# Fused attention and ResMLP: globals of the first two batches by indirect DMA, odd V chunks of batch 0 by VectorE, four score buffers, gated loads and a new order table

## The chip, the cores and the metric

The kernel runs on one core of one Trainium2 chip. The metric is the device time of one execution in microseconds: 402.45 us, the median of 4 runs (401.14 to 403.95). Below, PE is the matrix engine (TensorE), DVE VectorE, ACT ScalarE, POOL GpSimd and SP SyncE. All five run their own instruction streams in program order and wait for each other by semaphores. POOL, SP and ACT also issue DMAs.

## What is computed

8 batches, 8 heads, 576 tokens, head size 64. Attention is masked to a window of 32 tokens to each side, with 8 global tokens that see and are seen by all. Its result, heads side by side (512 wide), goes through a ResMLP block: a mix over tokens, then an MLP from 512 to 2048 to 512.

```python
scores = scale * np.matmul(q, k.transpose(0, 1, 3, 2))
mask = np.abs(pos[:, None] - pos[None, :]) <= window
mask = mask | is_global[:, None] | is_global[None, :]
attn = softmax(np.where(mask, scores, -1e9))       # in short
x = (attn @ v), heads side by side
...
a1 = alpha1 * x + beta1
tok = np.einsum('ts,bsd->btd', w_tok, a1)
u = x + lam * tok
a2 = alpha2 * u + beta2
ch = np.maximum(a2 @ w_ch1, 0.0) @ w_ch2
return (u + lam * ch).astype(np.float32)
```

## The kernel before

**Tiles.** Two heads make a head pair (hp 0 to 3). The tokens of a batch are five chunks of 128 (the last one 64). K sits transposed in `KT`, Q transposed and spread by head in `QP`, each with spare columns for the 8 globals. Scores are made in three units per head pair: matmuls `sc_mm` (L319), exponentials into `E` on ACT (`sc_exp`, L332), then on DVE the products with the masks: `probs_q` (L299) into `PGQ` (what the global rows need) and `probs_k` (L307) into `PT` (the window). `E` and `PT` have two buffers each, so head pair 2 waits for head pair 0. The products with V need V in two alignments: `Ve` holds chunks from token -32 on, `Vo` the same data moved by 64 tokens. `load_v` (L210) fills `Ve` by five DMAs on POOL, with a cast to fp16; `copy_vo` (L215 to L218) fills `Vo` from `Ve` by two SBUF to SBUF DMAs on SP. `gq_mm` (L347) multiplies `PGQ` with `Ve` for the globals, `gq_hi` and `gq_lo` put the result in `RG`. `pv_mms` (L369) then makes the outputs of a token tile from `G` and `RG`, from `PT` and `Ve`, and from `PT` and `Vo`. DVE normalises them into `XR` (L395), POOL (for one head pair DVE) scales them by alpha1*lam into `XL` (L413, L424, L425), and the token mix (L130 with `wtT`, L845, L841, L848) gives `UT`, the transposed input of the MLP.

**Globals.** For batches 0 and 1, `glob_mm` (L645) picks the 8 global K and Q columns of a head pair by ten small matmuls with a one-hot matrix `OH` (L769), and `glob_ev` (L653) copies them into `KGP` and `QP` on DVE. Later pairs of batches use `gather` (L243): an index column `hidx`, an indirect DMA on POOL for K and one for Q, `gather_x` (L249), a transpose (L253) and `gcols` (L231).

**Order of the work.** Batch 0 runs by the list `FIRST` (L45 to L54): each word names an entry of `ops` (L866 to L948), with a PSUM bank behind the colon where it is a group of matmuls, and is emitted in this order. Since each engine works in program order, this list sets the order on every engine, the DMA issues included. `kq1` in it (L857) puts on SP first `copy_vo(0)` and then the loads of K and Q of batch 1; `wi` (L728) puts the loads of w_tok and W1 on POOL, `b1i` (L743) those of the last 64 tokens of K and Q of batch 1 and of W2, `v1` (L749) those of V of batch 1. `W1s` starts the MLP. Behind the list come casts of batch 1 (L958 on POOL, L960 on DVE), `hidx` (L970) and two SP copies that fill `Vo[1]` (L1002, L1003).

Then 9 groups of the MLP follow, each 128 slots of one matmul with 512 columns (`mlp`, L515: 64 for W1, 64 for W2). `weave` (L87) puts the attention of the next batch between the slots, by weights; for batch 1 that is `first_attention` (L972) over slots 18 to 95, in which `w[hp]` are its products with `PT`, `Ve` and `Vo` and `q_[hp]` its `gq_mm`. Prefetches of batch g+2 (POOL DMAs) and DMA transposes (SP) hang on slots too.

Of the kernel before, what the change touches and what calls it, by code (L numbers as in the profile page):

```python
# [16 lines left out]
P = 128  # L17
# [28 lines left out]
i1 kgz qz1 ktz qz0 gb1 pgz gbm:0 gbc cq0 ck0 OH tk0:1 ar1 vez tq0:2 kt0 cq1 ck1 ptz qa0 tq1:3 qb0 tk1:4 qa1  # L46
qb1 Vi cq2 ck2 ar2 tq2:5 kt1 tk2:6 qa2 ck3 tt:7 kt2 cq3 kq1 gl0:0 ktt qtt tq3:1 ge0 qb2 gl2:2 qb3 qa3 wi s01:3
GM gl1:4 e01 tk3:6 s00:7 ge1 kt3 s02:5 e02 ge2 ab:0 s11:1 s12:3 e00 s10:4 abe gk1:6 e12 pgc mask e11 pt0 gk0:5
e10 fz eg1 pg1 pg0 eg0 q1:2 pt1 s21:7 ra1 s22:0 b1i q0:3 e21 G s20:1 ra0 s31:4 e20 s30:6 rd0 s32:5 e22 beta
pvx0:7 e31 pg2 pvy0:3 nx0 e32 wt2:1 e30 wt1:0 ny0 we2 pg3 q2:4 wt3:5 we1 pt2 q3:7 ra2 we3 wt4:6 LA1 rd2 ra3  # L50
wt0:3 xm0 we4 rd1 pvx2:1 rd3 we0 pvx1:0 xl0 nx2 pvy1:5 pvy2:4 nx1 xl2 rs:2 pt3 xl1 ny2 pvx3:7 re rf ny1 xm2
pvy3:6 tm0:3 ny3 xm1 v1 xm3 tm2:4 ad0 nx3 tm1:5 ru:2 rv ad2 xl3 tx0:6 ad1 tx2:3 ut0 tx1:7 ut2 tm3:4 ut1 wt5:1
ad3 we5 tx3:5 W1s ut3 beta1
# [4 lines left out]
def _consts():  # L58
# [19 lines left out]
    c32[:, 40:44] = 4 * p[:, None] + np.arange(4)[None, :]  # L78
    c32[:, 44] = np.where(p < 64, 512 + p, -1)
    c32[:, 45] = np.where(p >= 64, 448 + p, -1)  # L80
# [22 lines left out]
def kernel(ctx, tc, q, k, v, global_idx, alpha1, beta1, w_tok, alpha2, beta2, w_ch1, w_ch2, lam, out):  # L103
# [34 lines left out]
    OH = T("OH", [P, 6, 8], BF16)  # L138
# [56 lines left out]

    KST = XR[:, 4:8, :].rearrange("p a b -> p (a b)").rearrange("p (h j d) -> p h j d", h=H, j=4)
# [52 lines left out]
    def gather_x(i):  # L249
        for a in range(2):  # L250
            nc.vector.tensor_scalar(out=KQX[i][:, a, :], in0=KQG[i], scalar1=C32[:, 30 + a : 31 + a], scalar2=None, op0=ALU.mult)
# [47 lines left out]
    def probs_q(hp):  # L299
        e, pg = E[hp % 2], PGQ[hp]  # L300
        p1 = e.ap[0]
        gq_in = bass.AP(e.tensor, e.offset + 64, [p1, [272, 5], [72, 2], [1, 8]])
        gq_m = bass.AP(gqm.tensor, gqm.offset, [gqm.ap[0], [8, 5], [0, 2], [1, 8]])
        for c0 in (64, 96):
            nc.vector.tensor_tensor(out=pg[:, :, c0 : c0 + 16].rearrange("p c (a g) -> p c a g", a=2), in0=gq_in, in1=gq_m, op=ALU.mult)  # L305

    def probs_k(hp):  # L307
        e, pt = E[hp % 2], PT[hp % 2]
# [23 lines left out]
    def sc_exp(ps, hp, u):  # L332
        n = UOFF[u + 1] - UOFF[u]
        nc.scalar.activation(out=E[hp % 2][:, UOFF[u] : UOFF[u + 1]], in_=ps[:, 0:n], func=AF.Exp, bias=0.0, scale=0.125)  # L334

    def sc_unit(b, hp, u):
        def f():
            ps = sc_ps()
            sc_mm(ps, b, hp, u)
            sc_exp(ps, hp, u)  # L340
            if u == 2:
                probs_q(hp)
                probs_k(hp)

        return (0.6, f)
# [23 lines left out]
    def pv_mms(b, hp, i, o):  # L369
        par = b % 2  # L370
        gs = slice(128 * i, 128 * i + 128) if i < 4 else (slice(576, 704) if par == 0 else slice(512, 640))
        pt = PT[hp % 2]
# [272 lines left out]
    def glob_mm(ps, b, hp, n):  # L645
        for i in range(n):
            for m, st_ in enumerate((KB0, QB0[b])):
                o = ps[:, 16 * i + 8 * m : 16 * i + 8 * m + 8]
                for j in range(4):
                    mm(o, quad(st_, hp + i, j), OH[:, j, :], j == 0, False)  # L650
                mm(o, TSB[:, 128 * (hp + i) : 128 * (hp + i) + 128], OH[:, 4 + m, :], False, True)

    def glob_ev(ps, hp, n):  # L653
        v_ = ps[:, 0 : 16 * n].rearrange("p (i m) -> p i m", m=16)
        for a in range(2):
            r = slice(64 * a, 64 * a + 64)
            k0 = KGP[r, hp, 16 * hp + 8 * a : 16 * hp + 8 * a + 8]
            nc.vector.tensor_copy(out=bass.AP(KGP.tensor, k0.offset, [k0.ap[0], [P + 16, n], [1, 8]]), in_=v_[r, :, 0:8])
            q_, d0 = v_[r, :, 8:16], QP[r, hp, a, 0, 64:72]
            nc.vector.tensor_copy(  # L660
                out=bass.AP(QP.tensor, d0.offset, [d0.ap[0], [2 * NW * 72, n], [144, 5], [1, 8]]),
                in_=bass.AP(q_.tensor, q_.offset, [q_.ap[0], [16, n], [0, 5], [1, 8]]),
            )

    def glob(b, hp):
        def f():
            ps = pv_ps()
            glob_mm(ps, b, hp, 1)
            glob_ev(ps, hp, 1)

        return (0.5, f)
# [6 lines left out]
    g_.dma_start(out=C32, in_=nc.inline_tensor(c32n, name="c32_np").ap())  # L678
# [3 lines left out]
    ld_tail(k, TSB, g_, 0, 0)  # L682
    ld_tail(q, TSB, g_, 0, 64)
    nc.sync.dma_start(out=C16, in_=nc.inline_tensor(c16n, name="c16_np").ap())
    for t_, src in ((LA1, alpha1), (LAM, lam)):
        nc.sync.dma_start(out=t_, in_=src.unsqueeze(0).to_broadcast([P, DM]))
    for r in (64, 0):
        nc.sync.dma_start(out=LB[r : r + 1, :], in_=beta1.unsqueeze(0))
    nc.sync.dma_start(out=abr[0:4, :], in_=beta2.rearrange("(c p) -> c p", p=P))
    nc.sync.dma_start(out=abr[4:8, :], in_=alpha2.rearrange("(c p) -> c p", p=P))  # L690
    nc.sync.dma_start(out=ident, in_=nc.inline_tensor(np.eye(P, dtype=np.float32), name="ident_np").ap())
    nc.sync.dma_start(out=A2, in_=alpha2.unsqueeze(0).to_broadcast([P, DM]))
# [13 lines left out]
    def fill_pt(i):  # L706
        z = PT[i][:, 0, 0:64].bitcast(FP32)
        fill(bass.AP(z.tensor, z.offset, [z.ap[0], [608, 2], [64, 10], [1, 32]]), 0.0, g_)
# [6 lines left out]
    def ve_fill(i):  # L715
        fill(VF[i][0:32, 0:260], 0.0, g_)
        fill(VF[i][96:128, 1040:1300], 0.0, g_)
        fill(Ve[i][:, :, :, 64:65], 1.0, g_)
# [9 lines left out]
    def ld_w():  # L728
        g_.dma_start(out=WTB[:, 0:4, 0:S], in_=w_tok[0:512, :].rearrange("(c p) s -> p c s", p=P))
        g_.dma_start(out=WTB[0:64, 4, 0:S], in_=w_tok[512:S, :])  # L730
        ld_w1(0)
# [11 lines left out]
    def b1_begin():  # L743
        ld_tail(k, TSB, g_, 1, 0)
        ld_tail(q, TSB, g_, 1, 64)
        ld_w2(0)
# [9 lines left out]
    gb6 = bass.AP(gbc.tensor, gbc.offset, [gbc.ap[0], [0, 6], [1, 8]])  # L756
    gb9 = bass.AP(gbc.tensor, gbc.offset, [gbc.ap[0], [0, NW], [1, 8]])
    i6 = C32[:, 40:46]
# [9 lines left out]
    def onehot():  # L768
        nc.vector.tensor_tensor(out=OH, in0=bass.AP(i6.tensor, i6.offset, [i6.ap[0], [1, 6], [0, 8]]), in1=gb6, op=ALU.is_equal)  # L769

    def arith1():
        nc.vector.tensor_tensor(out=gsel, in0=gbc, in1=C32[:, 18:26], op=ALU.mult)
        nc.vector.tensor_reduce(out=gval, in_=gsel, axis=mybir.AxisListType.X, op=ALU.add)
# [33 lines left out]
    def wtok_tr(ps, k):  # L807
        ps = ps.bitcast(BF16)
        c0, n = (128 * k, 128 if k < 4 else 64) if k < 5 else (448, 128)
        cols = slice(c0, c0 + n)  # L810
# [4 lines left out]
    def wtok_ev(ps, k):  # L815
        ps, n = ps.bitcast(BF16), 64 if k == 4 else 128
        if k < 5:
            nc.scalar.copy(out=wtT[0:n, k, :], in_=ps[0:n, 0:S])
        else:
            nc.scalar.copy(out=wt4o[64:128, :], in_=ps[64:128, 0:S])  # L820
# [5 lines left out]
    def tok_sum_ev(ps, c0, n, odd):  # L826
        r, dst = (0, wt4o) if odd else (64, wtT[:, 4, :])
        nc.scalar.copy(out=dst[r : r + 1, c0 : c0 + n], in_=ps[r : r + 1, 0:n])
# [28 lines left out]
    def b1_kq():  # L857
        copy_vo(0)
# [6 lines left out]
    hb = {}  # L865
    ops = {  # L866
        "i1": lambda: None,
# [3 lines left out]
        "qz0": lambda: qzero(0, g_),  # L871
        "pgz": pg_zero,
        "vez": lambda: ve_fill(0),
        "ptz": lambda: (fill_pt(0), fill_pt(1)),
        "Vi": lambda: ld_v(0, 0, 5),
        "wi": ld_w,
        "fz": fills,
        "b1i": b1_begin,
        "v1": b1_v,
        "kq1": b1_kq,  # L880
# [3 lines left out]
        "OH": onehot,  # L884
# [11 lines left out]
        "gl0": lambda ps: glob_mm(ps, 0, 0, 1),  # L896
        "ge0": lambda: glob_ev(hb["gl0"], 0, 1),
        "gl1": lambda ps: glob_mm(ps, 0, 1, 1),
        "ge1": lambda: glob_ev(hb["gl1"], 1, 1),
        "gl2": lambda ps: glob_mm(ps, 0, 2, 2),  # L900
        "ge2": lambda: glob_ev(hb["gl2"], 2, 2),
# [6 lines left out]
        "re": lambda: tok_sum_ev(hb["rs"], 64, 512, False),  # L908
        "rf": lambda: tok_sum_ev(hb["rs"], 64, 512, True),
        "ru": lambda ps: tok_sum(ps, 0, 64),  # L910
        "rv": lambda: (tok_sum_ev(hb["ru"], 0, 64, False), tok_sum_ev(hb["ru"], 0, 64, True)),
# [4 lines left out]
    for h in range(HP):  # L916
        ops.update(
            {
                f"ck{h}": lambda h=h: cast_k(h, nc.scalar.copy),
# [4 lines left out]
                f"qa{h}": lambda h=h: pair_q(hb[f"tq{h}"], h, 0, nc.vector.tensor_copy),  # L924
                f"qb{h}": lambda h=h: pair_q(hb[f"tq{h}"], h, 1, nc.scalar.copy),
                f"pg{h}": lambda h=h: probs_q(h),
                f"pt{h}": lambda h=h: probs_k(h),
# [15 lines left out]
        for u in range(3):  # L943
            ops[f"s{h}{u}"] = lambda ps, h=h, u=u: sc_mm(ps, 0, h, u)
            ops[f"e{h}{u}"] = lambda h=h, u=u: sc_exp(hb[f"s{h}{u}"], h, u)
    for k_ in range(6):
# [10 lines left out]
    for hp in range(HP):  # L957
        cast_k(hp, g_.tensor_copy)  # L958
    for hp in range(HP):
# [10 lines left out]
    nc.vector.tensor_scalar(out=hidx, in0=C32[:, 26:30], scalar1=gval[:, 0:1], scalar2=None, op0=ALU.add)  # L970

    def first_attention(b):  # L972
        s = [[sc_unit(b, hp, u) for u in range(3)] for hp in range(HP)]
        t_ = [tr_pair(b, hp) for hp in range(HP)]
        g = [glob(b, hp) for hp in range(HP)]
# [106 lines left out]
```

The softmax here doesn't subtract the row's maximum and nothing guards it: scores larger than these inputs give would overflow.

## Time and profile before

| what | us |
|---|---|
| median of 4 runs | 402.45 (401.14 to 403.95) |
| the profiled execution: its own time | 402.77 |
| its span | 400.7 |
| PE busy | 376.1 (94%) |
| DVE busy | 229.9 (57%) |
| POOL busy | 212.6 (53%) |
| ACT busy | 169.0 (42%) |
| PE idle before matmuls on Vo, waiting for its DMA | 5.2 |
| start of the first MLP matmul | 47.75 |
| start of the first product with `Vo[1]` | 67.37 |

The span is the profiled execution from first to last instruction; its own time is about 2 us longer. In a line of the profile, `bank<-Vo,PT` means that a bank of PSUM is written from the tiles Vo and PT, `xN` counts instructions, L130 is the line of the one helper that issues most matmuls, and "<-DMA Vo<-Ve" names what ended an engine's idle time. In the slices each digit stands for a fortieth of the span, about 10 us, in tenths; `PEclk` is the clock that was granted to PE. In tables of stretches, a row gives the stretch, its length, and the busy time (and count) of PE, PE's weight loads, DVE, ACT and POOL, then PE's mean clock, the DMA share and GB/s. In timelines a row starts with the start and the length in us; "SPq" is the issue of a DMA on SP.

### The profile page before, as it was taken

The page shows a single profiled execution, that of the slowest core. Times are in us where ns is not written, and L with a number is a line of the kernel's source. Part 1 is how long each engine was busy: PE and PEld are TensorE (multiplying, and loading weights), DVE is VectorE, ACT ScalarE, POOL GpSimd, SP SyncE. Part 2 cuts the span into 40 slices and gives each one's busy share as a digit, 9 for nine tenths or more (in the row PEclk, how much of TensorE's full clock was granted, in tenths as well). Part 3 has the DMA queues.
Part 4 walks back from the last instruction along what each step waited for, and adds up shares of the span by engine and source line. Part 5 has one row for each costly group of instructions (what it writes and reads, how often), then busy time and mean ns, then how long its engine had stood idle before and what let it go on. Part 6 is the DMA issues. An engine that isn't in the chain of part 4 may idle for free.

```text
span 400.7 us, 8191 instructions
## 1 busy us (share of the span) xinstructions
PE 376.1 (94%) x3088; PEld 213.0 (53%) x3141; DVE 229.9 (57%) x615; ACT 169.0 (42%) x322; POOL 212.6 (53%) x282
## 2 busy tenths in 40 slices
PE   6548989997999999999999999999999999999996
PEld 3437756553665466545654665456546654444443
DVE  5547876868357755775478557744785464113013
ACT  4544377400880088008810880078108810640720
POOL 8834985627946883687457945884340335000000
PEclk9987999999999999999999999999999999999999
DMA  9999999994996999599949994999321003202002
GB/s 242 170 238 250 223 142 144 115 119 133 157 156 125 135 155 140 103 128 155 148 96 138 135 151 110 122 159 158 94 69 64 2 28 89 57 1 79 28 26 79
DMA packets 161628, 48.68 MB, mean 121 GB/s; under 512 B 147324, under 2 KB 154564, under 8 KB 161590
## 3 DMA queue, kind: packets, MB, share of 16 engines
q0 software_dynamic: 99840, 17.19, 66.0%
q1 hardware_dynamic: 60662, 29.93, 39.1%
q10 hardware_dynamic: 1088, 1.05, 0.9%
q8 instruction: 24, 0.39, 0.4%
q14 instruction: 14, 0.11, 0.1%
HBM read 39.31 MB, written 9.44 MB: 122 GB/s over the span
## 4 chain that ended last, share of the span: by engine, by line
PE 84%; DVE 5%; DMA 5%; POOL 3%; issue 2%; ACT 0%; SPq 0%; DVEq 0%; POOLq 0%; ACTq 0%
PE bank L130 82%; DMA Ve<-in_v_dram 2%; DMA Vo<-Ve 2%; DVE QP L605 1%; POOL Ve L213 1%; DVE PT L312 1%; DMA UT<-UB 1%; PE bank L813 1%; DVE XR L841 1%; DVE XR L395 0%; POOL PGQ L570 0%; DVE XR L543 0%; POOL Ve L570 0%; POOL TSB L587 0%; DVE OT L542 0%
## 5 line engine op out<-in xcount | busy, mean ns | idle before, releaser
L130 PE MATMUL bank<-UT,W 128*128 128x512 bf16 x546 | 152.8, 379 | 3.4 <-DMA UT<-UB 2.0
L130 PE MATMUL bank<-W,HT 128*128 128x512 bf16 (+2 forms) x572 | 138.0, 373 | 1.0 <-issue 0.2
L527 ACT ACTIVATE HT<-bank,bias 128x512 bf16<-128x512 f32 x128 | 87.8, 687 | 52.5 <-PE bank L130 51.6
L334 ACT ACTIVATE E<-bank 128x416 f16<-128x416 f32 (+1 forms) x96 | 47.2, 515 | 123.4 <-PE bank L130 122.6
L130 PEld LDWEIGHTS <-HT 128*128 128x128 bf16 x592 | 53.4, 98 | 52.6 <-issue 1.6
L413 POOL TENSOR_TENSOR XL<-XR,LA 128x384 bf16<-128x384 f32 x31 | 31.3, 1011 | 73.7 <-DVE XR L395 51.5
L130 PEld LDWEIGHTS <-W 128*128 128x128 bf16 x640 | 50.7, 97 | 28.8 <-issue 3.0
L542 DVE TENSOR_TENSOR OT<-bank,LAM 128x512 f32<-128x512 f32 (+2 forms) x37 | 24.9, 673 | 53.9 <-PE bank L130 53.6
L468 POOL TENSOR_TENSOR UB<-XR,A 128x512 bf16<-128x512 f32 x28 | 35.7, 1288 | 24.6 <-DVE XR L463 15.1
L130 PEld LDWEIGHTS <-PT 128*128 128x128 f16 x576 | 33.3, 99 | 24.4 <-DMA Vo<-Ve 5.3
L130 PE MATMUL bank<-RG,G 128*128 128x65 f16 x320 | 43.7, 194 | 1.2 <-DVE RG L356 0.7
L130 PE MATMUL bank<-Ve,PT 128*128 128x65 f16 x320 | 43.8, 196 | 0.0
L130 PE MATMUL bank<-Vo,PT 128*128 128x65 f16 x256 | 35.5, 194 | 6.1 <-DMA Vo<-Ve 5.2
L130 PE MATMUL bank<-XL,wtT 128*128 128x512 bf16 (+2 forms) x238 | 41.1, 326 | 0.1
L130 PEld LDWEIGHTS <-G 128*128 128x128 f16 x320 | 31.1, 98 | 14.3
L213 POOL DMA_DIRECT2D Ve<-in_v_dram x40 | 34.1, 868 | 4.3 <-PE bank L130 4.1
L130 PEld LDWEIGHTS <-KT 128*128 128x128 bf16 x288 | 24.5, 100 | 17.8 <-issue 1.4
L130 PE MATMUL bank<-QP,KT 128*128 128x144 bf16 (+1 forms) x288 | 33.0, 228 | 0.9 <-DVE QP L660 0.7
L543 DVE TENSOR_TENSOR XR<-OT,XR 128x512 f32<-128x512 f32 (+2 forms) x33 | 27.7, 840 | 1.6
L312 DVE TENSOR_TENSOR PT<-E,mask 128x640 f16<-128x640 f16 x64 | 28.4, 484 | 0.1
L395 DVE TENSOR_TENSOR XR<-bank,rd 128x384 f32<-128x384 f32 (+1 forms) x64 | 27.1, 424 | 2.3
L305 DVE TENSOR_TENSOR PGQ<-E,gqm 128x80 f16<-128x80 f16 x64 | 10.1, 200 | 31.4 <-ACT E L334 31.4
(137 smaller groups left out, 415.8 us busy)
## 6 DMA issues: line engine op xcount, KB each, us to landing
out_dram<-XR SPq DMA_DIRECT2D x31, 256.0 KB, 2.2
Vo<-Ve SPq DMA_DIRECT2D x16, 260.0 KB, 5.8
W<-in_moe_w_ch_dram POOLq DMA_DIRECT2D x4, 1024.0 KB, 24.0
Ve<-in_v_dram POOLq DMA_DIRECT2D x24, 128.0 KB, 8.8
Kb<-in_k_dram POOLq DMA_DIRECT2D x24, 128.0 KB, 5.4
Qb<-in_q_dram POOLq DMA_DIRECT2D x24, 128.0 KB, 6.0
Ve<-in_v_dram POOLq DMA_DIRECT2D x16, 96.0 KB, 3.8
XR<-in_q_dram ACTq DMA_DIRECT2D x4, 256.0 KB, 4.0
```

What stands on the lines that cost most here:

```text
L130: nc.tensor.matmul(out=o, lhsT=l, rhs=r, start=st, stop=sp, skip_group_check=True)
L213: nc.gpsimd.dma_start(out=Ve[b % 2][r0 : r0 + hi - lo, c, :, 0:D], in_=v[b, :, lo:hi, :].rearrange("h p d -> p h d"))
L305: nc.vector.tensor_tensor(out=pg[:, :, c0 : c0 + 16].rearrange("p c (a g) -> p c a g", a=2), in0=gq_in, in1=gq_m, op=ALU.mult)
L312: nc.vector.tensor_tensor(out=bass.AP(pt.tensor, pt.offset + 64 + 128 * par, [p0, [256, n], [1216, 2], [1, 64]]), in0=bass.AP(e.tensor, e. ...
L334: nc.scalar.activation(out=E[hp % 2][:, UOFF[u] : UOFF[u + 1]], in_=ps[:, 0:n], func=AF.Exp, bias=0.0, scale=0.125)
L395: nc.vector.tensor_tensor(out=xo, in0=pv[:, :, :, 0:64], in1=rb, op=ALU.mult)
L413: xl_eng(b, hp).tensor_tensor(out=XL[b % 2][:, 0:3, cs], in0=XR[:, base : base + 3, cs], in1=lb, op=ALU.mult)
L468: nc.gpsimd.tensor_tensor(out=ub, in0=x, in1=A2, op=ALU.mult)
L527: nc.scalar.activation(out=HT[:, ec, :], in_=st[ec], func=AF.Relu, bias=b_, scale=1.0)
L542: nc.vector.tensor_tensor(out=ot, in0=ps, in1=LAM[:, lo:hi], op=ALU.mult)
L543: nc.vector.tensor_tensor(out=x, in0=ot, in1=x, op=ALU.add)
L605: copy(out=QP[r, hp, a, 0:8, 0:64].rearrange("p t (u j) -> p t u j", j=4), in_=ps[r, 0:512].rearrange("p (j t u) -> p t u j", j=4, t=8),)
```

## The change

- **Globals of batches 0 and 1.** `OH`, `glob_mm` and `glob_ev` go. `hidx` is computed early (`arith0`), `gather(0)` issues the two indirect DMAs on POOL in batch 0's list, `gather_x` becomes one DVE operation with broadcasts for all columns, two fp32 transposes (`gt`) give K and Q columns, `glob_k` and `glob_q` put them in place for batch 0, and `glob_keep` (two ACT copies) keeps them for batch 1, which uses `gcols`. In `first_attention` the four `glob` entries become one `gcols(b)` at the front, with one gap changed.
- **V.** `copy_vo(0)` is not called for batch 0; two DVE copies (`voa`, `vob`) fill `Vo[0]`. `Vo[1]` keeps its two SP DMAs.
- **Four score buffers in batch 0.** `E0` and `PT0` have four entries, of which two lie in W2's first block and in columns of HT. W2's load therefore waits for their readers. All four head pairs have their own.
- **Loads.** The constants' table C32 is issued by SP instead of POOL, and the tails of K and Q come first on POOL. LA1, LAM, LB, alpha2, beta2 and A2 are loaded behind a POOL memset of LA1 that stands after the issue of V of batch 0; K and Q of batch 1 behind POOL memsets of their staging tiles. w_tok's load is split from W1's (`wki`, `wi`), the tails of batch 1 from W2's (`b1t`, `b1i`). The fp32 identity is cast by ACT instead of loaded.
- **Order.** `FIRST` is a new list: scores of head pairs 2, 0, 3, 1 before most of the rest; the casts of K of batch 1 (`kc`) stand on POOL before V of batch 1; some fills and evictions change engine (strings CK, QA, QB).
- **w_tok's odd tile** `wt4o` is copied by DVE (`wo`) from `wtT`, instead of a sixth group of transposes and ACT copies.

The diff, cut to its core:

```diff
 FIRST = """
-i1 kgz qz1 ktz qz0 gb1 pgz gbm:0 gbc cq0 ck0 OH tk0:1 ar1 vez tq0:2 kt0 cq1 ck1 ptz qa0 tq1:3 qb0 tk1:4 qa1
-qb1 Vi cq2 ck2 ar2 tq2:5 kt1 tk2:6 qa2 ck3 tt:7 kt2 cq3 kq1 gl0:0 ktt qtt tq3:1 ge0 qb2 gl2:2 qb3 qa3 wi s01:3
...
+vez kgz qz1 qz0 pgz gb1 ktz gbm:0 gbc idn ar0 ck0 ar1 gath tk0:1 cq0 kt0 cq1 tq0:2 ar2 ck1 tq1:3 tt:4 qb1 qb0
+Vi tk1:5 ck2 cq2 ktt qa0 tk2:6 qa1 tq2:7 qtt kt2 gx ck3 qb2 gt:0 kt1 cq3 tk3:1 qa2 ge0 tq3:2 gat1 kt3 pgc ge1
+qa3 qb3 s20:3 s02:4 ptz e20 s00:6 GM gk1:5 e02 e00 wki s30:7 voa eg1 s32:1 s22:2 mask e30 s12:3 s01:4 wi e22
+s10:6 e12 vob s21:5 e01 gk0:7 LA1 e10 pg0 fz s31:2 e21 s11:3 pt0 eg0 ab:4 q0:6 e32 pg2 ra0 G q2:5 ptz2 wt0:7
+e31 rd0 ra2 wt3:1 we0 beta b1t rd2 wt4:2 we3 pt2 pvy0:6 we4 wt1:7 ny0 gat2 pvy2:5 gte pg3 pvx2:1 xm0 e11 ny2
+q3:2 we1 wt2:6 pg1 xm2 ra3 pt1 q1:0 we2 pvx0:3 rd3 ra1 rs:5 nx2 rd1 xl2 nx0 pvx1:7 re pvy1:6 pt3 xl0 tm2:3 nx1
+b1i pvy3:2 ny1 tm0:5 ny3 xm1 ad2 pvx3:1 ad0 xl1 kc v1 tx2:7 nx3 tx0:6 xl3 tm1:3 xm3 abe tm3:5 ad1 ut0 ut2
+tx1:4 ad3 ut1 tx3:3 ut3 W1s ru:7 rv beta1 wo
 """
+    ew = W2.rearrange("p e d -> p (e d)").bitcast(FP16)
+    pw = HTt[:, 5 * S : 5 * S + 4864].bitcast(FP16)
+    E0 = E + [ew[:, 1232 * i : 1232 * i + 1232] for i in range(2)]
+    PT0 = PT + [pw[:, 2432 * i : 2432 * i + 2432].rearrange("p (a c) -> p a c", a=2) for i in range(2)]
...
     def gather_x(i):
-        for a in range(2):
-            nc.vector.tensor_scalar(out=KQX[i][:, a, :], in0=KQG[i], scalar1=C32[:, 30 + a : 31 + a], scalar2=None, op0=ALU.mult)
+        g, c = KQG[i], C32[:, 30:32]
+        nc.vector.tensor_tensor(
+            out=KQX[i],
+            in0=bass.AP(g.tensor, g.offset, [g.ap[0], [0, 2], [1, D]]),
+            in1=bass.AP(c.tensor, c.offset, [c.ap[0], [1, 2], [0, D]]),
+            op=ALU.mult,
+        )
...
+    def glob_tr(ps):
+        for i in range(2):
+            nc.tensor.transpose(out=ps[:, P * i : P * i + P], in_=KQX[i].rearrange("p a d -> p (a d)"), identity=ident)
+
+    def glob_keep(ps):
+        for i, t in enumerate((KGT, QGT)):
+            nc.scalar.copy(out=t[:, 0, :, :].rearrange("p b c -> p (b c)"), in_=ps[:, P * i : P * i + P])
...
-    g_.dma_start(out=C32, in_=nc.inline_tensor(c32n, name="c32_np").ap())
+    nc.sync.dma_start(out=C32, in_=nc.inline_tensor(c32n, name="c32_np").ap())
+    ld_tail(k, TSB, g_, 0, 0)
+    ld_tail(q, TSB, g_, 0, 64)
...
+    def ld_const():
+        fill(LA1[0:1, 0:1], 0.0, g_)
+        for t_, src in ((LA1, alpha1), (LAM, lam)):
+            nc.sync.dma_start(out=t_, in_=src.unsqueeze(0).to_broadcast([P, DM]))
...
     def b1_kq():
-        copy_vo(0)
+        fill(KST[0:1, 0, 0, 0:1], 0.0, g_)
+        fill(QST[0:1, 0, 0, 0:1], 0.0, g_)
         for h0 in (0, 4):
             ld_kq(k, KST, nc.sync, 1, h0, h0 + 4)
             ld_kq(q, QST, nc.sync, 1, h0, h0 + 4)
...
+    CK, QA, QB = "AAAA", "DAAA", "DADD"
...
+        "voa": lambda: V_.tensor_copy(out=Vo[0][0:64], in_=Ve[0][64:128, 0:4]),
+        "vob": lambda: V_.tensor_copy(out=Vo[0][64:128], in_=Ve[0][0:64, 1:5]),
+        "gat1": ld_const,
+        "wki": ld_wt,
         "wi": ld_w,
...
+        "kc": lambda: [cast_k(h, g_.tensor_copy) for h in range(HP)],
         "v1": b1_v,
-        "kq1": b1_kq,
+        "gat2": b1_kq,
+        "gath": lambda: gather(0),
...
-    for hp in range(HP):
-        cast_k(hp, g_.tensor_copy)
...
-        a = [t_[0], tr_tail(b), gap(0.5), t_[1], g[0], gap(0.5), g[1], gap(0.3), s[0][0], t_[2], gap(0.3), s[0][1], g[2], s[0][2], t_[3], gap(0.3)]
-        a += [s[1][0], g[3], s[1][1], s[1][2], gap(0.4)]
+        a = [(0.0, lambda: gcols(b)), t_[0], tr_tail(b), gap(0.5), t_[1], gap(0.8), s[0][0], t_[2], gap(0.3), s[0][1], s[0][2], t_[3], gap(0.3)]
+        a += [s[1][0], s[1][1], s[1][2], gap(0.4)]
```

## The prediction, made before the changed kernel ran

> **What bounds the kernel now.** I read the slices of the page first, then its chain, the waits and the chain of the first 75 us, SyncE's timeline, and a table of stretches. The slices and the chain's shares:
>
> ```profile
> PE   6548989997999999999999999999999999999996
> PEclk9987999999999999999999999999999999999999
> DMA  9999999994996999599949994999321003202002
> PE 84%; DVE 5%; DMA 5%; POOL 3%; issue 2%; ACT 0%; SPq 0%; DVEq 0%; POOLq 0%; ACTq 0%
> ```
>
> From about 70 us on TensorE is full, so only the front can change much: time won or lost before TensorE fills up goes to the end one for one. In the front the chain in order of time has
>
> ```profile
> 11.70 8.87 DMA Ve<-in_v_dram
> 20.72 0.54 SPq L217
> 21.36 8.11 DMA Vo<-Ve
> 29.52 1.61 PE bank L130 x26
> ```
>
> and the waits of the first 60 us have `PE bank L130 <- DMA Vo<-Ve` at 5.2 us. So V of batch 0 lands, SP copies it to Vo, and PE stands from 24.31 to 29.52. Both transfers are long because the DMA engines are crowded, not because they are big. Worse, the stall has a tail:
>
> ```profile
> 20.00:25.00 5.00, 4.22 (x47) 3.35 (x45) 4.60 (x15) 4.12 (x12) 3.38 (x6) 1.00 1.17 214
> 25.00:30.00 5.00, 0.48 (x9) 0.48 (x10) 0.08 (x1) 0.72 (x2) 0.00 (x0) 0.74 1.10 262
> 30.00:35.00 5.00, 5.00 (x54) 3.95 (x52) 3.62 (x13) 2.60 (x6) 1.34 (x3) 0.57 1.12 237
> ```
>
> (PE, PEld, DVE, ACT, POOL busy, then granted clock.) The clock records say 0.5 from 27.44 to 34.27. PE worked at half rate from 29.5 to 34.3: 4.8 us for 2.4 us of work. The stall's removal is thus worth up to 5.2 + 2.4 us at that place. But a second V follows, that of batch 1. SP's timeline:
>
> ```profile
> 58.37 0.47 SPq L1002 DMA_DIRECT2D Vo<-Ve  x1
> 58.93 0.70 SPq L1003 DMA_DIRECT2D Vo<-Ve  x1
> ```
>
> By the trace's semaphore updates V1's five chunks, issued by POOL at 42.80 to 47.04, land at 54.85 to 58.83; those two copies land at 64.67 and 66.83; the first matmul on Vo[1] starts at 67.37. That slack is only 0.5 us: the path through V1 and Vo[1] is almost as long as PE's.
>
> **What the Trainium skill says.** (1) "DMA: Bandwidth & Descriptors", "Issuing engines are not separate DMA queues": DMAs of all issuers run on the same 16 engines and interleave. The trace agrees: DMA is at 9 tenths in the first nine slices, and 260 KB of Vo[0] took 8.1 us from issue while W1 was under way. (2) The same page, "Queues, rings and completion order": each engine alternates between the queues that have work, and takes one queue's work in ring order. Agrees: POOL's V1 packets end after all of W2 (landed 53.46), which POOL issued earlier. (3) "TensorE: Matmul & The Clock Gate", Part 1: half rate after one idle window of about 3.4 us. Agrees: 0.5 from 3.1 us after the stall's start. (4) Price of the new copies, "VectorE: DVE Perf Modes", the perf-mode tier table: a 16-bit copy of 2048 elements is 0.693 us at 4x and 1.227 at 2x. No such copy is in the trace of before (nearest: QP's 64x576 copy, 0.445 us).
>
> **The front, part by part.** DVE copies voa and vob replace SP's two copies: 64x2080 fp16 each, by the price about 0.7 us each. Bounds 0.45 (nearest row, smaller) and 2.4 (no fast mode); I take 0.7, together +1.4 us of DVE.
> Globals: gather's indices (hidx) need gb1, gbm, gbc and three DVE operations, so they are ready near 7 us. POOL spends 1.07 + 0.99 us on the two indirect issues, as in rows of before. Behind them on POOL stand V0's five issues (0.87 each): about 9.2 to 13.9, where before they stood near 9.0 to 13.3. The landing needed is only gx/gt, long after; 7.9 us is the issue-to-landing of such a gather in before. Removed: 80 small matmuls of batches 0 and 1; batch 1's cost PE about 4 x 0.27 = 1.1 us before its first PV matmul. Fills and evictions that change engine lie beside loads that land at 11 us or later; they cost nothing unless DVE is late for the first casts, and then at most the 1.14 us of one QP fill. wt4o by two DVE copies instead of five transposes and an ACT eviction: 0.45 + 0.1 us, behind W1s, hidden.
> V0's packets begin about 13.0 instead of 12.5; chunk c3 lands near 20 (bounds 18.5 and 20.8; before 20.57). Then DVE goes through voa and vob 1.4, mask 0.75, LA1 0.68, eg1 and eg0 0.6, four pg 1.0, four pt 3.2, G 0.83, four rd 1.2, beta 0.68, four nx at 0.19+0.56 and four ny at 0.19+0.29+0.27, 6.0, head 3's xl and xm 1.0, abe 0.2, four ad 2.7: sum 20.2. One PT pair took 1.86 instead of 0.8 beside a busy POOL: +1.1. So the first MLP matmul starts at 20 + 21.3 = 41.3 us; before it was 47.75. Four score buffers keep PE and ACT ahead, so that DVE sets this pace. Gain at this place about 6.4 us (bounds 4 and 9). That is the step which the change visibly aims at.
>
> **Where the gain goes.** Batch 1's q matmuls (first readers of V1) came 65.37 - 47.75 = 17.6 us after the start of the MLP, its first PV 19.6 us. The globals' 1.1 us are gone, and the weave now puts the PV at slot 49 instead of 51.5: 2.5 slots at 0.216 us, 0.54 us that must then be done after it. PE so wants V1 at about 41.3 + 16.0 = 57.3 and Vo[1] at 41.3 + 17.9 = 59.2.
> When can they be there? I add the DMA engines' service. Mean packet times by size in the trace of before: V and tails (128 B) 17 ns, w_tok rows 100, W1 157, W2 80, K and Q of batch 1 52, broadcast constants 134, Vo 171. Times packets over 16 engines: V0 4608 packets 4.9 us; constants 3.2; w_tok 3.6; W1 1024 packets 10.05; K and Q 2048 packets 6.7; tails 1.1; Vo[0] 1.4; W2 2048 packets 10.2; V1 4.9.
> Before: from 12.5 on, with all but 1.7 us of the constants still to come: 4.9 + 1.5 + 3.6 + 10.05 + 6.7 + 1.1 + 1.4 + 10.2 + 4.9 = 44.3, end 56.8; measured 56.9. So the engines stand still nowhere in this stretch, and V1 is last in the sum. After: Vo[0]'s 1.4 are out, but all constants are gated to behind V0: 4.9 + 3.2 + 3.6 + 10.05 + 6.7 + 1.1 + 10.2 + 4.9 = 44.6 from 13.0, end 57.6, 0.7 later than before. A front that computes faster doesn't move V1, for it stands behind the same bytes. Its last chunk lands near 59.5, the copies issue at 59.1 and 59.6 (they stay DMAs and POOL's next prefetch competes as before), land near 65.4 and 67.5.
> So PE waits some 2 us for V1 and then, after the q matmuls and two MLP slots, about 6 us for Vo[1], and starts the PV near 67.55 instead of 67.37: +0.2. Plus 0.54 of slots. Plus a restart at half clock after 6 us of standing, like that of before: +2.4. Sum +3.1: 402.77 + 3.1 = 405.9 for a profiled execution (span 400.7, 2.1 around it); the median lies 0.3 below that execution: **405.5 us**.
>
> **New waits.** W2's issue on POOL now stands behind pt3 and exps (score buffers lie in W2's memory, probabilities in HT). I reckon pt3 at about 34 us; the sum above needs W2's packets from about 38 on. Queued behind on POOL: xm1, xl1, the four K casts, V1, the next gather, K and Q of batch 2. The K casts (0.62 each) moved ahead of V1's issue and wait for K of batch 1: before it landed at 41.36, so V1 is issued near 44.6 to 48.9, while its packets have their turn only near 52.7. Each margin is about 4 us. The gates on LA1 (a POOL memset behind V0's issue) and on K and Q of batch 1 cost memsets of some 0.1 us; what stands behind the latter on SP is nothing before Vo[1].
>
> **Rivals.**
> A, likeliest, 0.58: as above; V1 and Vo[1] take the gain, 405.5, own range 401.5 to 409.
> B, faster, 0.22: V1 and Vo[1] come in time, since the DMA sum is smaller than I think or Vo[1] meets an emptier queue. Then the PV starts at 59.2: 67.37 - 59.2 - 0.54 = 7.6 us less, 394.9; with Vo[1] at 63 it is 399. For it: 1.4 us of Vo[0] are gone, and the gathers hold little. Against it: the closed sum up to 56.9.
> C, slower, 0.20: W2 stands behind pt3 on POOL too long. It decides once pt3 ends after about 38 us; from there W2, V1, Vo[1] and the end are late by one us for each us, so with 4 to 5 us about 410. The same way goes a K of batch 1 that lands after 45 (then V1's issue is late).
> That the globals or the scores of batch 0 are not faster at all: contained in the lower bound of the gain; it then has no stall at Vo[1] and ends within 1% of before.
>
> **How the numbers follow.** The time is A's. Measurement of this kernel tells about 1% (4 us) from no change: faster means below 398.4, slower above 406.5. B gives 0.20 below 398.4 with a little from A's low edge; A gives 0.18 above 406.5 and C 0.17; the rest is 0.45. The range from 397 to 409.5 leaves out B's lower part (0.12) and C's upper part (0.08).
>
> **What would show it.** Right: no PE wait on Vo near 24 us and full clock from 25 to 35; first MLP matmul at 41; V1 landing at 57.5 to 59.5; new PE waits on Ve and Vo near 58 to 67; half clock near 67 to 71. Wrong: Vo[1] landed before 63, or PE not waiting for it, gives B; a POOL wait at W2's issue on DVE PT that ends after 38, gives C; an MLP start later than 45 says that DVE's walk was mis-sized.

## The result, and the profile after

The changed kernel takes 405.2 us (median of 33 runs, 402.31 to 407.56) against 401.95 us for the kernel before beside it (54 runs). The ratio is 1.0079, with a 95% interval of 1.0066 to 1.0093: slower by 0.8%. Its profiled execution has a span of 403.0 us, against 400.7.

The slices and the chain's shares of the changed kernel's page:

```profile
PE   5849886999999999999999999999999999999995
PEclk9977999899999999999999999999999999999999
DMA  9999999992995999599949994999521003102002
PE 80%; DMA 8%; POOL 5%; DVE 4%; issue 2%; SPq 0%; POOLq 0%
```

PE's dent in the third slice (20 to 30 us) is still there, and there is a new one in the seventh. DMA's share of the chain rose from 5% to 8%. PE's longest waits in the first 110 us:

```profile
PE bank L819 <- DMA HT<-in_moe_w_tok_dram: 3.9, 1, 3.9
PE bank L127 <- DMA Vo<-Ve: 3.3, 1, 3.3
```

The chain of the first 80 us, in order of time (start, length, what):

```profile
17.10 10.99 DMA HT<-in_moe_w_tok_dram
28.14 0.23 PE bank L819
...
49.03 11.84 DMA Ve<-in_v_dram
61.01 0.55 SPq L1015
61.66 6.52 DMA Vo<-Ve
68.23 2.78 PE bank L127 x28
```

The wait for Vo near 24 us is gone, but PE now stands from 24.24 to 28.14 for w_tok (its load lies in HT's memory, hence the name). After that comes the path through V and Vo of batch 1: V's last chunk landed at 61.22 (before 58.83), and Vo[1] at 68.19 (66.83). The same stretches as before, then the two that hold the second stall:

```profile
20.00:25.00 5.00, 2.13 (x24) 1.54 (x21) 3.94 (x13) 3.35 (x9) 4.32 (x11) 1.00 1.02 140
25.00:30.00 5.00, 1.86 (x14) 1.29 (x15) 1.56 (x4) 0.98 (x2) 0.00 (x0) 0.52 1.14 218
30.00:35.00 5.00, 5.00 (x65) 4.41 (x64) 3.80 (x14) 3.10 (x8) 2.55 (x4) 0.50 1.11 237
...
57.00:67.00 10.00, 7.65 (x64) 4.89 (x62) 5.09 (x15) 7.27 (x16) 9.23 (x12) 1.00 2.14 150
67.00:80.00 13.00, 11.49 (x122) 7.32 (x125) 6.08 (x20) 4.77 (x10) 7.23 (x11) 0.87 1.97 143
```

PE did 2.1 us of work from 20 to 25 where it did 4.2 before, and its clock stood at a half from 25.17 to 35.41, 10.2 us instead of 6.8. The first MLP matmul starts at 46.52, 1.2 us earlier than before. Then PE stands for Vo[1] from 64.93 to 68.23 and works at half clock from 69.54 to 72.96. The first product with Vo[1] is at 68.23, against 67.37.

Why w_tok is late shows in the DMA view from 17 to 22 us, queue rows with packets, MB and share. First the changed kernel:

```profile
DMA packets 415, 0.67 MB, mean 135 GB/s; under 512 B 76, under 2 KB 98, under 8 KB 415
q1 hardware_dynamic: 370, 0.65, 95.7%
q0 software_dynamic: 45, 0.02, 3.3%
```

and the kernel before in the same stretch:

```profile
DMA packets 2507, 0.91 MB, mean 183 GB/s; under 512 B 1972, under 2 KB 2464, under 8 KB 2506
q0 software_dynamic: 2478, 0.85, 170.0%
q1 hardware_dynamic: 28, 0.04, 2.8%
```

(Shares above 100% show that the records of an engine's packets overlap.) POOL's queue (q0) holds next to nothing here in the changed kernel: V of batch 0 had ended at 17.2, and w_tok, issued at 16.35, had its first packet only at 21.38. Until then the engines carry the gated constants alone; their packets of 2 KB took a mean of 239 ns (before, among other packets, 157), and the last of them starts at 23.6. Before, V's packets ran to 19.8 and covered w_tok's 4.5 us from issue to first packet, and the constants had run beside V.

The 5.0 us from w_tok's issue to its first packet are no fixed latency of this load. In the version of experiment 5 that loads the constants at the start again, w_tok is issued at nearly the same time (16.22) and its first packet comes 1.6 us later. In the eight traces that load the constants at the start, or issue them only behind w_tok, w_tok's first packet comes 1.0 to 2.2 us before V's last has ended; in the four that have the gated constants ahead of w_tok it comes 1.8 to 4.2 us after V's last. So w_tok's load is late while these constants are being moved; by what mechanism, no run shows.

### The profile page after: what moved, and what is told of

It is laid out like the page before. It is cut to its first block, busy times and chain, and to the rows that moved or that the text cites. A ratio compares the mean times of both kernels' runs of the same rounds, so it can differ in the third digit from the quotient of the medians.

```text
span 403.0 us, 8006 instructions
## 1 busy us (share of the span) xinstructions
PE 376.7 (93%) x3006; PEld 212.4 (53%) x3058; DVE 231.3 (57%) x596; ACT 168.1 (42%) x322; POOL 213.2 (53%) x284
## 4 chain that ended last, share of the span: by engine, by line
PE 80%; DMA 8%; POOL 5%; DVE 4%; issue 2%; SPq 0%; POOLq 0%
PE bank L127 80%; DMA Ve<-in_v_dram 3%; DMA HT<-in_moe_w_tok_dram 3%; POOL Ve L220 2%; DMA Vo<-Ve 2%; POOL UT L593 1%; DMA UT<-UB 1%; DVE XR L407 1%; DVE XR L555 1%; POOL KQG L252 1%; DVE OT L554 0%; PE bank L821 0%; DVE XR L475 0%; DVE PGQ L317 0%; DVE HT L324 0%
## 5 line engine op out<-in xcount | busy, mean ns | idle before, releaser
L346 ACT ACTIVATE E<-bank 128x416 f16<-128x416 f32 (+1 forms) x90 | 44.6, 516 | 120.7 <-PE bank L127 120.0
L127 PEld LDWEIGHTS <-HT 128*128 128x128 bf16 (+1 forms) x628 | 55.8, 99 | 52.8 <-issue 1.6
L480 POOL TENSOR_TENSOR UB<-XR,A 128x512 bf16<-128x512 f32 x28 | 35.8, 1288 | 23.6 <-DVE XR L475 15.7
L127 PE MATMUL bank<-RG,G 128*128 128x65 f16 x320 | 44.8, 196 | 1.2 <-DVE RG L368 0.6
L127 PEld LDWEIGHTS <-PT 128*128 128x128 f16 x540 | 31.7, 99 | 21.1 <-DMA Vo<-Ve 3.4
L127 PE MATMUL bank<-Ve,PT 128*128 128x65 f16 x300 | 42.1, 196 | 0.0
L127 PE MATMUL bank<-Vo,PT 128*128 128x65 f16 x240 | 33.9, 194 | 3.3 <-DMA Vo<-Ve 3.3
L127 PE MATMUL bank<-QP,KT 128*128 128x144 bf16 (+1 forms) x288 | 31.9, 226 | 0.5 <-ACT E L346 0.2
L213 POOL DMA_DIRECT2D Kb<-in_k_dram x30 | 27.2, 906 | 3.8 <-PE bank L127 3.0
L400 DVE RECIPROCAL rd<-bank 128x6 f32<-128x6 f32 (+1 forms) x64 | 11.9, 186 | 29.6 <-PE bank L127 29.1
L127 PEld LDWEIGHTS <-wtT 128*128 128x128 bf16 (+1 forms) x240 | 18.6, 99 | 18.5 <-issue 2.6
```

Source lines behind the costliest of these rows:

```text
L127: nc.tensor.matmul(out=o, lhsT=l, rhs=r, start=st, stop=sp, skip_group_check=True)
L213: nc.gpsimd.dma_start(out=dst[0:n, c, :].rearrange("p (h d) -> p h d", d=D), in_=src[b, :, c * P : c * P + n, :].rearrange("h p d -> p h d"))
L346: nc.scalar.activation(out=eb(b, hp)[:, UOFF[u] : UOFF[u + 1]], in_=ps[:, 0:n], func=AF.Exp, bias=0.0, scale=0.125)
L400: nc.vector.reciprocal(out=rt[:, 0 : 2 * n], in_=ps[:, 0 : 130 * n].rearrange("p (i e) -> p i e", e=65)[:, :, 64:65].rearrange("p i o -> p ...
L480: nc.gpsimd.tensor_tensor(out=ub, in0=x, in1=A2, op=ALU.mult)
```

## Experiments

The ratios are against the kernel before, run beside each.

**1. One part of the change alone, in the kernel before: Vo[0] by VectorE.** The K and Q loads of batch 1 get a gate, since Vo's copies on SP had held them back.

```diff
-qb1 Vi ... kt2 cq3 kq1 gl0:0 ktt
+qb1 Vi ... kt2 cq3 gl0:0 ktt
-... s22:0 b1i q0:3 e21 G s20:1
+... s22:0 b1i kq1 q0:3 e21 voa vob G s20:1
     def b1_kq():
-        copy_vo(0)
+        fill(KST[0:1, 0, 0, 0:1], 0.0, g_)
+        fill(QST[0:1, 0, 0, 0:1], 0.0, g_)
```

> The kernel before with one part of the change alone: Vo[0] by two VectorE copies (ahead of G in the order list), and K and Q of batch 1 gated by two tiny POOL memsets behind W2's issue, so that they start about when they did. Theory (V and Vo of batch 1 bind): PE's 5.2 us wait for Vo[0] shrinks to about 1 and the half clock after it goes, the first MLP matmul comes 4 to 7 us earlier than 47.75, but V of batch 1 lands near 57 to 58 (Vo[0]'s 1.4 us of DMA service gone) and PE then stands for Vo[1]: time 0 to 2 us under the kernel before, 399.5 to 402. Rival (the front passes to the end): 394 to 397.

Measured: 399.73 us, ratio 0.9974 (0.9956 to 0.9993). The first MLP matmul starts at 42.81, 4.9 us earlier, with no half clock after 23.2. The chain ahead of the first PV of batch 1 has

```profile
40.44 15.24 DMA Ve<-in_v_dram
56.47 8.03 DMA Vo<-Ve
```

and PE's waits have

```profile
PE bank L130 <- DMA Vo<-Ve: 2.0, 1, 2.0
```

V was issued 5 us earlier and landed only 2.5 us earlier (56.35, where I expected 57 to 58), behind W2. So 4.9 us in the front were worth 1.6 us at the end. This shows that transfers of batch 1 take most of what the front gains, and that the VectorE copies (with the gate on K and Q) are a small gain by themselves, not the loss.

**2. The same part undone in the changed kernel: Vo[0] by SP's DMAs.**

```diff
-        "voa": lambda: V_.tensor_copy(out=Vo[0][0:64], in_=Ve[0][64:128, 0:4]),
+        "voa": lambda: nc.sync.dma_start(out=Vo[0][0:64], in_=Ve[0][64:128, 0:4]),
...
```

(and `vob` likewise.)

> The changed kernel with Vo[0] filled by two SP DMAs again instead of VectorE's two copies: that part of the change alone undone. Theory: the DMA lands near 25 to 27, ahead of w_tok at 28.1 and of the first product with Vo[0] near 30.5, so that it is hidden: the first MLP matmul within 1 us of 46.5; its 1.4 us of DMA service stand in front of V of batch 1: 405 to 406.5. Rival (the VectorE copies are worth the 5.2 us stall that the kernel before had): 408 or more.

Measured: 405.74 us, ratio 1.0100 (1.0064 to 1.0135). Vo[0] landed at 28.60, w_tok at 29.01; PE stood 4.5 us for w_tok and none for Vo[0]:

```profile
PE bank L819 <- DMA HT<-in_moe_w_tok_dram: 4.5, 1, 4.5
```

The time is not told apart from the changed kernel's. The first MLP matmul was at 48.56 in this trace, 2.0 us later than in the changed kernel's, where I had expected at most 1. So in the changed kernel w_tok's wait covers the wait that the VectorE copies were made to remove.

**3. Vo[1] by VectorE in the changed kernel.**

```diff
-    nc.sync.dma_start(out=Vo[1][0:64], in_=Ve[1][64:128, 0:4])
-    nc.sync.dma_start(out=Vo[1][64:128], in_=Ve[1][0:64, 1:5])
+    def vo1_copy():
+        nc.vector.tensor_copy(out=Vo[1][0:64], in_=Ve[1][64:128, 0:4])
+        nc.vector.tensor_copy(out=Vo[1][64:128], in_=Ve[1][0:64, 1:5])
...
-... s[2][0], s[2][1]] + w[0] + ...
+... s[2][0], s[2][1], (0.0, vo1_copy)] + w[0] + ...
```

> The changed kernel with Vo[1] filled by two VectorE copies just ahead of the first products that need it, in place of SP's two DMAs. Theory (the DMA copy's 6.5 us from issue to landing is the last link): V lands near 61.2 as before, the copies take 0.7 us each, PE does not wait at 64.9: 400 to 401.5. Rival (V itself is the last link and VectorE's queue holds PE instead): 403 to 405.

Measured: 401.17 us, ratio 0.9995 (0.9981 to 1.0009). Compared by the ratios, this is 3.4 us less than the changed kernel, with the front as late as there (first MLP matmul at 47.42) and V landing at 62.42. VectorE's timeline, and PE's wait:

```profile
65.90 0.88 DVE L987 COPY Vo<-Ve 64x2080 f16<-64x2080 f16 x1
66.81 0.74 DVE L988 COPY Vo<-Ve 64x2080 f16<-64x2080 f16 x1
...
PE bank L127 <- DVE Vo L988: 1.3, 1, 1.3
```

The copies are done 1.6 us after VectorE starts them, where SP's DMAs took 6.5 us from issue to landing, and PE waits 1.3 us instead of 3.3. The clock stays full after 33.5. Between the two profiled executions (404.76 us and here 402.38) the first product with Vo[1] came 0.6 us earlier (67.60), though V landed 1.2 us later, and the 1.7 us of the second half clock are gone; together that is 2.3 of the 2.4 us. So the DMA copy and the half clock behind it are worth as much as the loss against the kernel before. They are not the only term of that path, since experiment 5 recovers more with the DMA copy in place.

**4. V of batch 1 issued in front of W2.**

```diff
-... we4 wt1:7 ny0 gat2 pvy2:5 gte ...
+... we4 wt1:7 ny0 gat2 v1 pvy2:5 gte ...
-... ad0 xl1 kc v1 tx2:7 ...
+... ad0 xl1 kc tx2:7 ...
```

> The changed kernel with V of batch 1 issued on POOL in front of W2 (behind the gates of K and Q of batch 1). Theory (the V behind W2's bytes binds): V lands near 50 and Vo[1] near 56, PE's 3.3 us before the first product with Vo[1] and the half clock from 69.5 to 73 (1.7 us) are gone: 400 to 401. Rival (the time was lost in the front, by the wait for w_tok and its half clock; the Vo[1] stall would only be replaced by a wait for W2 or K of batch 1): 404 to 406.

Measured: 405.49 us, ratio 1.0088 (1.0059 to 1.0117). The theory missed. The time lies in the rival's range, but the trace shows another reason than the rival's. POOL's timeline:

```profile
28.28 1.75 POOL L220 DMA_DIRECT2D Ve<-in_v_dram  x2 [0.91 <-DMA HT<-in_moe_w_tok_dram]
36.07 0.78 POOL L220 DMA_DIRECT2D Ve<-in_v_dram  x1 [6.04 <-DMA W<-in_moe_w_ch_dram]
36.95 0.48 POOL L436 TENSOR_TENSOR XL<-XR,LA 128x128 bf16<-128x128 f32 x1
```

POOL stood 6 us before V's last issue; the trace names a landing of W1 as what ended it. That too many loads were outstanding is my reading, which no run tests. Batch 0's scalings behind it came late, so that the first MLP matmul started at 53.66 instead of 46.52. V landed at 51.89 and Vo[1] at 59.65, and PE did not wait for either. A front 7.1 us later without the second stall thus costs about the same as the early front with it. I had not counted the wait of the issue itself.

**5. Constants and w_tok, together and apart.** The first edit loads the constants at the start again; the second puts w_tok's load behind V of batch 0.

```diff
     def ld_const():
-        fill(LA1[0:1, 0:1], 0.0, g_)
...
+    ld_const()
     nc.scalar.activation(out=b2c[:, 0:1], in_=zero, ...
-... tq3:2 gat1 kt3 pgc ge1
+... tq3:2 kt3 pgc ge1
```

```diff
-Vi tk1:5 ck2 ...
+Vi wki tk1:5 ck2 ...
-... e02 e00 wki s30:7 voa ...
+... e02 e00 s30:7 voa ...
```

Both:

> The changed kernel with w_tok's load issued on POOL directly behind V of batch 0, and the constants loaded at the start again (no gate). In the changed kernel PE stood 3.9 us for w_tok, which landed at 28.1. Theory (V and Vo of batch 1 bind the end; the front is late because w_tok is): w_tok lands near 24 to 25.5, the first MLP matmul starts near 43 instead of 46.5, but the product with Vo[1] moves only by what the DMA engines gain from the constants' earlier place, 1 to 2.5 us, and PE's stall before it grows from 3.3 to 5 us or more; time 403 to 404.5. Rival (the front passes through to the end one for one): 401.5 or less.

Constants only:

> The changed kernel with the constants loaded at the start again (no gate), w_tok's load left where the change put it (the other half). Theory: the DMA engines have the constants out of the way while they wait for work, V of batch 1 lands near 57 to 58 instead of 61.2, Vo[1] near 64.5 to 65.5: 401 to 402.5. Rival: the gate is worth little, 404 or more.

w_tok only:

> The changed kernel with w_tok's load directly behind V of batch 0 on POOL, the constants still gated (one half of the earlier run with both). Theory (what helps the end is that the constants no longer take DMA time between V of batch 0 and W1): w_tok lands near 25.5 to 26.5, first MLP matmul near 44 to 45, but V of batch 1 and Vo[1] come as in the changed kernel less about 1 us: 403.5 to 405. Rival (w_tok's lateness in the front is what was paid): 401 to 402.

| version | us (median) | ratio to before, 95% interval | profiled execution, us | w_tok landed | first MLP matmul | V of batch 1 landed | PE's wait for Vo[1] |
|---|---|---|---|---|---|---|---|
| changed kernel | 405.2 | 1.0079 (1.0066 to 1.0093) | 404.76 | 28.09 | 46.52 | 61.22 | 3.30 |
| both | 400.79 | 0.9972 (0.9951 to 0.9994) | 398.95 | 23.30 | 43.67 | 56.95 | 1.91 |
| constants only | 398.77 | 0.9963 (0.9929 to 0.9997) | 398.78 | 23.23 | 44.94 | 56.34 | 0.85 |
| w_tok only | 403.51 | 1.0056 (1.0036 to 1.0076) | 401.38 | 23.97 | 47.56 | 59.29 | 0.48 |

The gate on the constants is the costly part of the change. Without it the ratio falls by 1.1 to 1.2 points, some 4.5 us (the eight runs of "constants only" spread from 398.54 to 402.86, so its ratio is above that of the medians). V of batch 1 lands 4.3 and 4.9 us earlier, and the first product with Vo[1] comes 4.2 us earlier (63.98 and 64.07), where I had put 1 to 2.5 us on record; no second half clock follows. Both times are below the range of their theory, and that of "both" is in its rival's (401.5 or less). The rival's reason, that the front passes one for one, doesn't fit: the front came 2.9 and 1.6 us earlier, the product 4.2. The versions "both" and "constants only" aren't told apart: their intervals overlap.

The DMA view of "constants only" from 17 to 22 us, to set beside the two above:

```profile
DMA packets 1576, 0.76 MB, mean 151 GB/s; under 512 B 1033, under 2 KB 1572, under 8 KB 1576
q0 software_dynamic: 1576, 0.76, 132.4%
```

Here V and w_tok follow each other, and W1's first packet comes at 21.88 instead of 24.90. The same 386 packets of constants, now beside K, Q and V, took a mean of 92 ns each.

The columns from the fourth on come from one execution of each version, and executions differ. Versions with the same front had the first MLP matmul at 43.67 ("both") and 46.43 (the first version of experiment 6), so a difference under 3 us in that column shows nothing by itself. The landing of V is firmer: 56.34 to 58.51 in the four traces of the changed kernel without the gate, 61.22 to 62.42 in the three (changed kernel, experiments 2 and 3) with the gate and w_tok where the change put it.

With w_tok moved alone, a gain isn't shown, for the interval overlaps the changed kernel's; the profiled execution was one of its fastest (its runs took 400.91 to 405.52). In it w_tok landed 4 us earlier but the first MLP matmul did not come earlier. PE had a new wait:

```profile
PE bank L859 <- DMA abr<-in_moe_alpha_dram: 3.0, 1, 3.0
```

Here the gated constants themselves were late. That half of the expectation (44 to 45) was wrong, while its time was in the range.

**6. The best of each side.** First the changed kernel with w_tok early, constants at the start and Vo[1] by VectorE; then the same without moving w_tok; then the kernel before with both Vo by VectorE (the edits of 1 and 3).

> The changed kernel with w_tok directly behind V of batch 0, the constants at the start, and Vo[1] by two VectorE copies. Theory (both are terms of one path: the bytes ahead of V of batch 1, then the copy): V lands near 57, no wait of PE for Vo[1] worth over 0.7 us, so the gained front passes: 397.5 to 399.5. Rival (a new wait, for K and Q of batch 1, W2 or a VectorE behind its copies, takes it): 400.5 or more.

> The changed kernel with the constants at the start and Vo[1] by VectorE copies, w_tok's load where the change put it. Theory: the 0.85 us wait for Vo[1] that was left goes or becomes a VectorE wait of the same size: 397.5 to 399.5. Rival (the rest of the change is worth several us once its transfers are out of the way): 396 or less.

> The kernel before with Vo[0] and Vo[1] by VectorE copies (the earlier run with Vo[0] alone, plus the second pair in place of SP's DMAs). Theory: the 1.96 us that PE stood for Vo[1] there go and nothing takes their place but a VectorE queue of up to 1 us: 397.5 to 399, which is no worse than any version of the changed kernel, so that globals by DMA, four score buffers and the new list bring nothing of their own here. Rival (the copy's DMA was only covered by V's landing): 399.5 or more.

Measured: 399.44 us, ratio 0.9950 (0.9929 to 0.9972); 397.79 us, 0.9895 (0.9866 to 0.9924); 396.85 us, 0.9866 (0.9834 to 0.9898). The first two are in their ranges, the last is below its own. So w_tok's early load brings nothing on top; the first is slower than the second, for a reason that stays open. The last has the lowest median of all, 1.3% under the kernel before, with none of the change's globals, score buffers, gates on constants or list. Its first MLP matmul is at 41.76, and PE's waits have

```profile
PE bank L130 <- DVE Vo L977: 1.2, 1, 1.2
```

where its DMA version (experiment 1) had 2.0 for Vo. The first product with Vo[1] comes at 62.76 instead of 64.55. These 1.8 us are less than the 4.3 us between the two ratios; the rest isn't assigned. Beside it, the repaired changed kernel (397.79) is not better: the intervals overlap. So no run shows a gain of globals by DMA, four score buffers and the new list; each by itself was not tried.

## Why the prediction was right, and where not

**The mechanism at the end: right, and shown.** The prediction had the gain of the front end in a new wait for Vo[1], a start of its first product at 67.55, and a restart at half clock. It was 68.23, with half clock from 69.54 to 72.96. The terms: start +0.86 (forecast +0.2), half clock 1.7 (forecast 2.4); the 0.54 of slots is worked out and not measured. With it the sum is 3.1, as forecast. But the two profiled executions differ by 2.0 (402.77 and 404.76, where 405.9 was forecast) and their spans by 2.3, so about 1 us of that sum isn't in the trace's total; the medians beside each other differ by 3.2. Experiments 1 and 3 show the mechanism from both sides.

**The front: wrong.** Forecast was a first MLP matmul at 41.3; it was 46.52, outside the stated bounds. The step that failed is DVE's walk without a stop from V's landing on:

```profile
21.78 0.69 DVE L914 TENSOR_TENSOR LA<-LA,LAM 128x512 f32<-128x512 f32 x1 [0.97 <-DMA LAM<-in_moe_lam_dram]
31.07 0.18 DVE L400 RECIPROCAL rd<-bank 128x4 f32<-128x4 f32 x1 [4.45 <-PE bank L127]
```

The walk's work was right: from the first copy at 18.60 to 46.52 VectorE was busy 21.5 us (forecast 21.3). But it stood 4.45 us (26.6 to 31.07) for PE, which stood for w_tok and then worked at half clock, 0.97 us for the constant LAM and 1.0 us in smaller pauses. That is more than the 1.4 us by which the walk began earlier than forecast: V's c3 landed at 17.40, below my lower bound of 18.5, with nothing beside most of it any more (19.74 where the constants were back at the start). I had costed the gate on the constants as a memset of 0.1 us and some bytes in a sum, and the later place of w_tok not at all; neither as something that PE or VectorE waits for. So the sign that I had named, a start after 45 for a walk of the wrong size, pointed the wrong way. The two copies took 0.70 us each, as priced from the Trainium skill's "VectorE: DVE Perf Modes", section "The perf-mode tier table", for a 16-bit copy of about this length at 4x; the trace agrees. (The 1.227 us at 2x that I quoted beside it stands in the table's 32-bit column; nothing rested on it.)

**The sum of DMA service: right in kind, too small.** It gave 44.6 us from V's first packet to V1's last; the trace has 11.53 to 60.45, 48.9. The constants were mis-sized: 3.2 us in the sum, 5.8 us (386 packets at 239 ns on 16 engines) when they ran mostly alone, and no other load's packets filled the engines from 17.2 to 21.4, though w_tok and W1 had been issued. V of batch 0 took 5.65 us instead of 4.9. These two make at most 3.4 of the 4.3 us: the sum's 134 ns for a packet of constants is below their recorded mean before, 157 ns, which gives 3.8 us, and its other packet times are likewise 7 to 20 ns below the recorded means (17 against 35 for V, 157 against 173 for W1). The rest I cannot assign. Because both the front and V came later than forecast, PE's stall was 3.3 us and not 8, and the end came out nearly the same. The time was hit in part because two errors offset each other.

**Rival C: its condition held, its effect isn't shown.** W2's issue stood behind the score buffers until 38.83, past the 38 that I had named. But W2's first packet started 1.6 us after W1's last, against 1.2 in the kernel before, so by this gap some 0.4 us can be put down to it. In the traces without the gate the gap is 3.7 to 4.6 us, against 1.6 to 2.1 in the kernel before with VectorE copies, and W2 is issued there at 35.7 to 37.6 instead of 20.5 to 20.7. Whether this is why the repaired changed kernel isn't better, no run tries; tails of K and Q lie in the gap too. Experiment 4 did not settle this, since POOL's own stall covered it.

**Rival B** was the right size for what the kernel could have gained: without the constants' gate and with Vo[1] by VectorE the front does pass, to 397.8 (B had 394.9, or 399 with Vo[1] at 63; the first product came at 64.11).

## What to carry to other kernels

When a stall at the front goes, look for the next transfer of the same kind, here V and its shifted copy one batch later, and ask whether it stands behind the same bytes: it decides what the first repair is worth. A load that is gated "in order of need" still has to be moved: here the constants took 2.2 us of the engines' time beside other loads at the start and 5.8 us alone behind V, and w_tok and W1, issued behind them, came late. So look at what a gate puts the load in front of, and not only at its bytes. A small SBUF to SBUF copy on the end's path is worth trying on an engine that has time: here the two halves of Vo[1] took 7.2 us by DMA from the first issue to the last landing, of which their packets make 2.0 us on 16 engines, and 1.6 us on VectorE. And when several parts of a change come together, add the likely winner alone to the kernel before: here that was the best version.

## What the runs showed of the hardware

Constants broadcast to 128 partitions took a mean of 239 to 257 ns per 2 KB packet when they ran mostly alone (four traces with the gate) and 92 to 157 ns among other packets (the other eight); W1's packets of the same size took 173 in the changed kernel and before. A 260 KB copy from SBUF to SBUF, as for Vo[0] and Vo[1], took some 6 to 8 us by DMA, from issue to landing, under load (8.1 for Vo[0] before, 6.5 for Vo[1] in the changed kernel), and 0.70 to 0.88 us for the same bytes on VectorE. The load of w_tok, 576 packets issued by POOL behind V, had its first packet 1.0 to 2.2 us before V's last had ended in eight traces, and 1.8 to 4.2 us after it in the four with the gated constants ahead of it. V of batch 0 had its own first packet 1.7 us after its issue in the changed kernel.
